# Attention and a routed expert layer on one Trainium2 core: list weights behind first products, three routing buffers, four small gate products, and a new order

## The chip, the cores and the metric

The kernel runs on one core of one Trainium2 chip. The metric is the device time of one execution in microseconds (us). The engines are TensorE (PE), VectorE (DVE), ScalarE (ACT), GpSimd (POOL) and SyncE (SP), which issues DMA transfers; each runs its own list of instructions in a fixed order and waits for others by semaphores.

## The reference, cut to what matters

```
a = softmax(phi, over the sequence)                 # 8 batches, 8 heads, 576 tokens, 32 memory slots
k_m, v_m = a^T k, a^T v
x = softmax(q k_m^T / 8) v_m                        # x: 4608 tokens x 512
noisy = x Wg + log1p(exp(x Wn)) * noise             # 8 experts
top2 and softmax of their two values
for each expert e, each of its tokens t:
    out[t] += weight[t, e] * relu(x[t] W1[e]) W2[e]   # W1 512 x 1024, W2 1024 x 512
```

## The kernel before, in words

The 64 batch-heads are 16 units of one batch and four heads (`unit`, `a_load` to `a_v`): load phi, k and v, form exp, k_m and v_m, and scores of q. Batches go in four pairs P0 to P3 of 1152 tokens, nine tiles of 128 rows and five groups n each (`JS`, `group`). A group is put through transposes (`c_sc`), softmax (`c_soft1`, `c_soft2`; L396 is the last multiply, by 1/sum), transposes (`c_tr`) and the products with v (`c_av`), which leave a tile of x in `xr`; ACT copies it from PSUM (L419) and SP writes it to a DRAM buffer `xs` (L423). The same product brings the gate logits as 16 more columns: `a_g` has multiplied each unit's v by the gate's weights (L318), masked the result to the diagonal blocks of the four heads (L320) and summed it over the heads (L322).

When a pair is complete, `gate` (P3 in two parts, five tiles and four) finds each token's two experts on DVE (to `gmb`, L474), counts places in the experts' lists by products on PE (L480 to L485), turns these into `gidx` (L502), has POOL number the tokens (iota, L495) and DVE the weights in `gent`, and scatters one list entry a token and choice to the DRAM list `lst`: 72 scatters on POOL (L514), 18 a pair, the last pair 10 and 8. A list read (L593, on SP) waits for the scatters of the pairs that it needs.

Experts then run over their lists: POOL gathers 128 rows of x (`gtile`, L640), ACT and DVE split them into two f16 halves (`ghalf`, L651 and L654, a ring of two buffers), SP transposes them by DMA (L655). `mm1` makes the first products (L678, PSUM ring `mp` of three), ACT the relu `r` (L684), DVE the halves hh and hl (L685, L686). `mm2` makes the second products (L705, L715), ACT scales them by the list weights `wlu` to `y` (L709), and POOL adds them to `out` (L728), which SP has zeroed in 38 writes (L150). Weights are loaded (L544), measured (`wam`, L555), scaled (`wsc`) and split into halves wh and wl (L569, L570).

Expert 0 has groups g0, g1 (two tiles each, which need only P0 and P1), g2 (two tiles, needs P2) and (0,3) (four tiles, the last of 64 entries, needs all lists). They run while attention still does; experts 1 to 7 follow in groups of 4, 4 and 2 tiles. `wt` makes `wlu`: L617 for whole tiles, L621 for the 64 entries.

The order of work before (0,3) comes from a list of tasks sorted by times that the table `PRI` gives; a scheduler places instructions of each engine by these. `BUF` holds ring sizes, and numbers that tie an instruction behind a named product (`after`). Behind it the program's own order of calls counts. What stands first on an engine runs first; nothing passes a waiting instruction on its engine.

## Time and profile before

| | |
|---|---|
| median of 3 runs | 1042.14 us (1041.88 to 1044.54) |
| profiled execution, its own time | 1048.34 us |
| its span | 1046.5 us |
| mean granted clock of TensorE, share of full speed | 0.958 |
| busy in the span: PE, DVE, ACT, POOL | 92%, 51%, 35%, 29% |
| chain that ended last, by engine | PE 56%, DMA 8%, issue 6%, DVE 6%, POOL 2% |

The span runs from the first to the last instruction that the profile shows; the execution's own time is 1.8 us longer. A row of a timeline gives the start and the length of an instruction (or of several alike), and in brackets how long its engine stood idle before and what ended that. A window's row gives each engine's busy time in a stretch. Idle time of an engine matters only if the chain passes through it.

### The profile page before, as it was taken

Reading aid. Unit: us, or ns where it says so; the run is one execution under the profiler, and the core shown is the slowest. Engines: PE = TensorE matmul, PEld = TensorE weight load, DVE = VectorE, ACT = ScalarE, POOL = GpSimd, SP = SyncE. Lnnn points to the kernel's source line nnn. Section 1 sums busy time; section 2 is a strip of 40 time slices with the busy share of each in tenths; the row PEclk is TensorE's granted clock in tenths of the full one; section 3 lists DMA queues with packets and bytes.
Section 4 is the critical chain, followed back from the end, with each engine's and each line's share of the span. In section 5 each row is a group of like instructions: output and inputs, shape, how many; then the busy total and the mean of one; then the engine's idle time right before and its main releaser. Section 6 shows DMA issues by size and latency. Waiting matters only on the chain.

```text
span 1046.5 us, 15053 instructions
## 1 busy us (share of the span) xinstructions
PE 962.7 (92%) x5632; PEld 500.4 (48%) x5632; DVE 535.2 (51%) x1395; ACT 370.5 (35%) x760; POOL 298.4 (29%) x262
## 2 busy tenths in 40 slices
PE   4898975895799998999999999999999999999995
PEld 3555643563344445444644464445444544454452
DVE  2578888535476254984272349544523682232211
ACT  3466655313242232532242244324222542221211
POOL 1000633776246304222323132223132213211121
PEclk9699977798899999999999999999999999999998
DMA  9999999555988439756546257845453626430221
GB/s 291 331 327 327 267 330 302 113 118 84 238 148 196 95 37 176 204 129 100 107 131 110 42 91 206 170 88 82 131 101 78 124 57 110 66 51 11 31 32 25
DMA packets 143642, 147.93 MB, mean 141 GB/s; under 512 B 92944, under 2 KB 102224, under 8 KB 143568
## 3 DMA queue, kind: packets, MB, share of 16 engines
q1 hardware_dynamic: 124112, 107.02, 39.9%
q0 software_dynamic: 19456, 39.93, 22.0%
q8 instruction: 45, 0.74, 0.3%
q14 instruction: 29, 0.24, 0.1%
HBM read 86.77 MB, written 40.22 MB: 121 GB/s over the span
## 4 chain that ended last, share of the span: by engine, by line
PE 56%; DMA 8%; issue 6%; DVE 6%; POOL 2%; ACT 1%; SPq 0%; POOLq 0%; ACTq 0%; DVEq 0%
PE mp L678 27%; PE ps L705 27%; DMA xt<-ghalf 3%; DVE wl L570 2%; DMA lst<-gent,gidx 2%; DVE wam L555 2%; PE ps L715 2%; DMA stg<-in_w 2%; DMA out<-y,lt 1%; POOL out L728 1%; POOL lst L514 1%; DVE ghalf L654 1%; DVE hl L686 0%; ACT ghalf L651 0%; DVE hh L685 0%
## 5 line engine op out<-in xcount | busy, mean ns | idle before, releaser
L678 PE MATMUL mp<-xt,wh 128*128 128x512 f16 (+2 forms) x1408 | 280.2, 336 | 11.3 <-issue 6.6
L678 PEld LDWEIGHTS <-wh 128*128 128x128 f16 x1600 | 152.5, 99 | 143.6 <-issue 26.6
L728 POOL DMA_INDIRECT out<-y,lt x80 | 128.7, 1609 | 259.8 <-ACT y L709 231.9
L705 PE MATMUL ps<-wh,hl 128*128 128x512 f16 x528 | 200.0, 379 | 1.6 <-DVE hl L686 1.6
L705 PE MATMUL ps<-wl,hh 128*128 128x512 f16 x528 | 199.8, 379 | 0.0
L685 DVE CAST hh<-r 128x512 f16<-128x512 f32 (+3 forms) x200 | 72.1, 364 | 248.8 <-ACT r L684 247.7
L705 PE MATMUL ps<-wh,hh 128*128 128x512 f16 x528 | 195.5, 379 | 1.3 <-DVE hh L685 1.3
L640 POOL DMA_INDIRECT gtile<-xs,lt x80 | 91.0, 1138 | 332.5 <-DVE ghalf L654 292.0
L684 ACT ACTIVATE r<-mp 128x512 f32<-128x512 f32 (+3 forms) x200 | 97.0, 492 | 246.9 <-PE mp L678 175.4
L705 PEld LDWEIGHTS <-hh 128*128 128x128 f16 x1152 | 112.3, 98 | 135.1 <-DVE hh L685 4.6
L678 PE MATMUL mp<-xt,wl 128*128 128x512 f16 (+2 forms) x704 | 151.4, 337 | 0.0
L654 DVE TENSOR_TENSOR ghalf<-gtile,ghalf 128x512 f16<-128x512 f32 x80 | 55.1, 691 | 126.1 <-ACT ghalf L651 125.9
L686 DVE TENSOR_TENSOR hl<-r,hh 128x512 f16<-128x512 f32 (+3 forms) x200 | 111.3, 562 | 4.6
L651 ACT ACTIVATE ghalf<-gtile 128x512 f16<-128x512 f32 x80 | 50.0, 628 | 170.7 <-DMA xt<-ghalf 155.6
L514 POOL DMA_INDIRECT lst<-gent,gidx x72 | 73.0, 1014 | 129.3 <-DVE pe L385 102.8
L678 PEld LDWEIGHTS <-wl 128*128 128x128 f16 x800 | 76.9, 99 | 58.6 <-issue 1.3
L705 PEld LDWEIGHTS <-hl 128*128 128x128 f16 x576 | 56.3, 98 | 74.7 <-issue 5.7
L555 DVE TENSOR_REDUCE wam<-stg 128x1 f32<-128x512 f32 x128 | 81.1, 678 | 20.4 <-DMA stg<-in_w 20.2
L709 ACT ACTIVATE y<-ps,wlu 128x512 f32<-128x512 f32 x66 | 44.7, 681 | 125.0 <-PE ps L705 92.0
L570 DVE SCALAR_TENSOR_TENSOR wl<-stg,wsc,wh 128x512 f16<-128x512 f32 x112 | 76.4, 743 | 1.9 <-ACT wh L569 1.7
L569 ACT ACTIVATE wh<-stg,wsc 128x512 f16<-128x512 f32 x112 | 70.1, 708 | 14.2 <-DVE wsc L336 13.8
L417 PE MATMUL xp<-vb,at 128*128 128x272 f32 (+1 forms) x160 | 50.6, 477 | 14.7 <-ACT xr L419 14.0
(160 smaller groups left out, 723.2 us busy)
## 6 DMA issues: line engine op xcount, KB each, us to landing
stg<-in_w SPq DMA_DIRECT2D x64, 512.0 KB
kvs<-in_kv SPq DMA_DIRECT2D x16, 1024.0 KB
out<-zt SPq DMA_DIRECT2D x38, 256.0 KB
qs<-in_q_t SPq DMA_DIRECT2D x16, 576.0 KB
xs<-xr SPq DMA_DIRECT2D x36, 256.0 KB
phs<-in_phi_t SPq DMA_DIRECT2D x16, 288.0 KB
kvs<-in_kv SPq DMA_DIRECT2D x16, 128.0 KB
gtile<-xs,lt POOLq DMA_INDIRECT x80
```

Of the source, the lines that this page charges most:

```text
L514: sc = G.indirect_dma_start(out=lst[:, :], out_offset=bass.IndirectOffsetOnAxis(ap=idx[:, j, k:k + 1], axis=0), in_=ent[:, j, k, :], in_of ...
L555: d = V.tensor_reduce(am[:, c:c + 1], ss[c], axis=AX.X, op=OP.max, apply_absolute_value=True)
L569: A.activation(wh[:, cs], ss[c], AF.Identity, scale=sc)
L570: V.scalar_tensor_tensor(wl[:, cs], ss[c], sc, wh[:, cs], op0=OP.mult, op1=OP.subtract)
L640: G.indirect_dma_start(out=gts[i][:n], out_offset=None, in_=xs[0:seen, :], in_offset=bass.IndirectOffsetOnAxis(ap=LT[e][:n, t, 0:1].bitcas ...
L654: V.tensor_tensor(gh[:n, 1], gts[i][:n], gh[:n, 0], OP.subtract)
L678: d = mark["mm1", g if e == 0 else None] = T.matmul(ps[:, :n], ww[:, c * FF + f * 128:c * FF + (f + 1) * 128], xt[:, xo + c, :n], start=(k ...
L684: A.activation(r[:, :n], ps[:, :n], AF.Relu, scale=HC)
L685: V.tensor_copy(hh[:, f, :n], r[:, :n])
L686: V.tensor_tensor(hl[:, f, :n], r[:, :n], hh[:, f, :n], OP.subtract)
L705: T.matmul(ps, hs[:, i * 128:(i + 1) * 128], ws, start=(k == 0), stop=(k == 8 * m - 1))
L728: d = G.indirect_dma_start(out=out[:, :], out_offset=bass.IndirectOffsetOnAxis(ap=LT[e][:n, t, 0:1].bitcast(I32), axis=0), in_=y[:n], in_o ...
```

## The change

The table `PRI` and some numbers of `BUF` are set anew, and the ring of gathered tiles has four buffers, not three. `a_g` makes four products of 32 rows by 16 columns, one for each head, side by side in one PSUM tile, and ACT copies the result; DVE's mask and sum go. The last multiply of the softmax is on GpSimd for the first five groups (`GL` and `GV` are zero, so their branches change nothing). `gidx` and `gent` have three buffers, not one. `early_wt`'s tie behind the first product of its group now holds for all tiles of expert 0, and the list weights of (0,3) are made behind that group's first products, not before its gathers. Line numbers of the changed kernel are 2 to 7 higher.

```diff
-PRI = dict(D=5.51308, p=-3.88947, kv=-1.28633, q=-2.43825, exp=-1.09034, tr1=-2.82213, tr5=-2.85978, kvm=0.71326,
...
+PRI = dict(D=5.82512, p=-2.56477, kv=-1.63998, q=-2.4532, exp=-1.09005, tr1=-2.82213, tr5=-2.85978, kvm=0.91616,
...
-           ws=1, m0=16, m1=18, m2=19, r0=6, r1=6, zr=5)
+           ws=1, m0=15, m1=18, m2=19, r0=14, r1=3, zr=6)
-GT = 3
+GT = 4
+GN, GL, GV = 5, 0, 0
@@ a_g
-        T.matmul(p4[:, 0, 0:64], VT[u], wg_sb[:, g, :], start=True, stop=True)
-        gt = sm.tile([128, 4, 16], F32, name="gt")
-        V.tensor_tensor(gt, p4[:, 0, 0:64].rearrange("p (h c) -> p h c", h=4), vmask[:, :, 0:16], OP.mult)
         vb = wk.tile([128, 272], F32, name="vb", bufs=8)
-        V.tensor_reduce(vb[:, 256:], gt.rearrange("p h c -> p c h"), axis=AX.X, op=OP.add)
+        for h in range(4):
+            T.matmul(p4[h * 32:(h + 1) * 32, 0, 0:16], VT[u][:, h * 32:(h + 1) * 32],
+                     wg_sb[:, g, h * 16:(h + 1) * 16], start=True, stop=True)
+        A.activation(vb[:, 256:], p4[:, 0, 0:16], AF.Copy)
@@ c_soft2
-        V.tensor_tensor(pe[:, 0:k], pe[:, 0:k], ss[:, 0:k, None].to_broadcast([128, k, M]), OP.mult)
+        (G if n < GN else V).tensor_tensor(pe[:, 0:k], pe[:, 0:k], ss[:, 0:k, None].to_broadcast([128, k, M]), OP.mult)
@@ gate
-        idx = gs.tile([128, NJ, 2], I32, name="gidx")
-        ent = gs.tile([128, NJ, 2, 2], F32, name="gent")
+        idx = gs.tile([128, NJ, 2], I32, name="gidx", bufs=3)
+        ent = gs.tile([128, NJ, 2, 2], F32, name="gent", bufs=3)
@@ wt
-        if e == 0 and t1 <= 6:
+        if e == 0:
             after(d, "mm1", t0 // 2)
@@ the main sequence
     lists(0, 6, NTL + 1)
-    wt(0, 6, NTL + 1)
...
         for f in range(8):
             mm1(e, g, f)
             step_side(2)
+        if (e, g) == (0, 3):
+            wt(0, 6, NTL + 1)
```

**POOL, from ahead of P2's scatters to P3's last.** Before:

```order
L495 IOTA gent 128x18
L640 DMA gtile<-xs,lt 128x512 x3
L514 DMA lst<-gent,gidx 37888x2 x13
L640 DMA gtile<-xs,lt 128x512
L514 DMA lst<-gent,gidx 37888x2 x5
L495 IOTA gent 128x10
L514 DMA lst<-gent,gidx 37888x2 x10
L728 DMA out<-y,lt 4864x512
L640 DMA gtile<-xs,lt 128x512 x2
L728 DMA out<-y,lt 4864x512
L495 IOTA gent 128x8
L514 DMA lst<-gent,gidx 37888x2 x8
```

After the change (L520 is the scatter, L646 the gather, L734 the add to `out`):

```order
L501 IOTA gent 128x8
L646 DMA gtile<-xs,lt 128x512 x4
L520 DMA lst<-gent,gidx 37888x2 x28
L646 DMA gtile<-xs,lt 128x512 x2
L734 DMA out<-y,lt 4864x512 x2
L520 DMA lst<-gent,gidx 37888x2 x8
L646 DMA gtile<-xs,lt 128x512 x3
```

P2's 18 scatters and the first 10 of P3 stand in one run behind four gathers; the gather in P2's scatters and the iotas between them are gone from there.

**SP, around the first list reads** (L150 zero writes, L423 and L429 x tiles, L593 and L599 list reads). Before:

```order
L150 DMA out<-zt 128x512 x5
L423 DMA xs<-xr 256x1x256 x2
L150 DMA out<-zt 128x512
L423 DMA xs<-xr 256x1x256
L150 DMA out<-zt 128x512 x2
L593 DMA lt<-lst 128x2x2 x2
L423 DMA xs<-xr 256x1x256 x2
L655 DMA_TRANSPOSE stg<-ghalf 128x8x128 x2
```

After the change:

```order
L152 DMA out<-zt 128x512
L429 DMA xs<-xr 256x1x256
L152 DMA out<-zt 128x512
L599 DMA lt<-lst 128x2x2 x2
L152 DMA out<-zt 128x512 x4
L429 DMA xs<-xr 256x1x256
L152 DMA out<-zt 128x512 x2
L429 DMA xs<-xr 256x1x256 x4
L661 DMA_TRANSPOSE stg<-ghalf 128x8x128 x2
```

The list reads stand ahead of the last six zero writes and of four x tiles that they stood behind.

**ACT and DVE, in g1 and g2.** ACT before, from g1's r's to the first r's of g2 with the first two halves of (0,3) (L684 and L690 are r, L651 and L657 halves, L709 and L715 y, L569 wh):

```order
L684 ACTIVATE r<-mp 128x256 x7
L651 ACTIVATE ghalf<-gtile 128x512
L684 ACTIVATE r<-mp 128x256
L651 ACTIVATE ghalf<-gtile 128x512
L709 ACTIVATE y<-mp,wlu 128x512 x2
L569 ACTIVATE wh_3813<-stg,wsc 128x512 x3
L684 ACTIVATE r<-mp 128x256
L569 ACTIVATE wh_3813<-stg,wsc 128x512 x5
L651 ACTIVATE ghalf<-gtile 128x512
L684 ACTIVATE r<-mp 128x256
L651 ACTIVATE ghalf<-gtile 128x512
L684 ACTIVATE r<-mp 128x256 x4
```

ACT after the change, from g2's first half on:

```order
L657 ACTIVATE ghalf<-gtile 128x512
L690 ACTIVATE r<-mp 128x256
L657 ACTIVATE ghalf<-gtile 128x512
L690 ACTIVATE r<-mp 128x256 x3
L575 ACTIVATE wh_3829<-stg,wsc 128x512 x8
L690 ACTIVATE r<-mp 128x256 x3
L657 ACTIVATE ghalf<-gtile 128x512 x2
L715 ACTIVATE y<-mp,wlu 128x512 x2
L690 ACTIVATE r<-mp 128x256
L657 ACTIVATE ghalf<-gtile 128x512
L690 ACTIVATE r<-mp 128x256
L657 ACTIVATE ghalf<-gtile 64x512
```

g2's two halves follow r 9 and r 10, and the halves of (0,3) stand ahead of g1's y's and among the first r's of g2. DVE after the change, at the end of g1's halves (L627 are the list weights of the 64 entries, L660 the halves of gathered tiles, L691 and L692 hh and hl):

```order
L691 CAST hh<-r 128x256 x2
L692 TENSOR_TENSOR hl<-r,hh 128x256 x2
L691 CAST hh<-r 128x256
L627 TENSOR_SCALAR wlu<-lt,wu 64x1
L692 TENSOR_TENSOR hl<-r,hh 128x256
L660 TENSOR_TENSOR ghalf<-gtile,ghalf 128x512 x2
L691 CAST hh<-r 128x256
L692 TENSOR_TENSOR hl<-r,hh 128x256
L660 TENSOR_TENSOR ghalf<-gtile,ghalf 128x512
```

The 64 entries' weights, which stood behind DVE's scale chain, now stand ahead of g1's last hl.

## Rows read from the trace of the kernel before

**Rows 1.** The page, part 1: engine, busy us, share, instructions.

```profile
PE 962.7 (92%) x5632; PEld 500.4 (48%) x5632; DVE 535.2 (51%) x1395; ACT 370.5 (35%) x760; POOL 298.4 (29%) x262
```

**Rows 2.** Table of windows: length, busy us of each engine (instructions), PEclk, DMA share, GB/s.

```profile
150.00:175.00 25.00, 18.19 (x85) 10.66 (x82) 22.93 (x78) 17.31 (x41) 14.90 (x15) 0.88 1.07 299
196.05:208.60 12.55, 12.55 (x106) 10.58 (x107) 8.33 (x46) 3.05 (x10) 9.51 (x10) 0.85 0.52 69
208.60:219.40 10.80, 10.80 (x60) 5.11 (x59) 4.45 (x26) 1.91 (x5) 6.51 (x8) 1.00 0.27 32
325.00:1046.00 721.00, 704.25 (x3728) 343.79 (x3726) 327.58 (x675) 225.37 (x397) 177.54 (x132) 1.00 0.50 97
```

**Rows 3.** Timeline of PE: start, us, line, operation, [idle before <-releaser].

```profile
24.61 1.43 PE L275 MATMUL tr<-kvs,es 128*32 128x128 f32 x40 [0.76 <-DMA kvs<-in_kv]
...
255.65 1.01 PE L678 MATMUL mp<-stg,wh 128*128 128x256 f16 x4 [5.61 <-ACT r L684]
...
285.60 1.65 PE L678 MATMUL mp<-xt,wh 128*128 128x448 f16 x4 [6.65 <-issue]
```

**Rows 4.** Timeline of POOL, 168 to 254 us.

```profile
168.01 0.97 POOL L514 DMA_INDIRECT lst<-gent,gidx  x1 [0.30 <-issue]
...
184.83 1.00 POOL L640 DMA_INDIRECT gtile<-xs,lt  x1 [9.79 <-DMA lt<-lst]
...
188.66 1.00 POOL L514 DMA_INDIRECT lst<-gent,gidx  x1 [0.30 <-issue]
...
214.73 0.14 POOL L495 IOTA gent<- 128x10 int32 x1 [1.79 <-DMA lst<-gent,gidx]
...
228.46 1.62 POOL L728 DMA_INDIRECT out<-y,lt  x1 [0.30 <-DMA lst<-gent,gidx]
...
246.14 1.62 POOL L728 DMA_INDIRECT out<-y,lt  x1 [0.30 <-issue]
253.28 1.01 POOL L640 DMA_INDIRECT gtile<-xs,lt  x1 [5.51 <-DMA lt<-lst]
```

**Rows 5.** Timeline of SP (its DMA queue), 179 to 268 us.

```profile
179.30 1.09 SPq L593 DMA_DIRECT2D lt<-lst  x2
...
189.71 3.26 SPq L655 DMA_TRANSPOSE stg<-ghalf  x2
...
247.81 10.50 SPq L593 DMA_DIRECT2D lt<-lst  x16
...
261.07 6.45 SPq L655 DMA_TRANSPOSE xt<-ghalf  x2
```

**Rows 6.** Timeline of ACT, the halves of gathered tiles.

```profile
194.79 0.63 ACT L651 ACTIVATE ghalf<-gtile 128x512 f16<-128x512 f32 x1 [1.42 <-DMA stg<-ghalf]
...
258.56 0.61 ACT L651 ACTIVATE ghalf<-gtile 128x512 f16<-128x512 f32 x1
...
271.03 0.63 ACT L651 ACTIVATE ghalf<-gtile 128x512 f16<-128x512 f32 x1 [5.79 <-DMA xt<-ghalf]
...
275.80 0.63 ACT L651 ACTIVATE ghalf<-gtile 64x512 f16<-64x512 f32 x1 [3.59 <-DMA xt<-ghalf]
```

**Rows 7.** Timeline of DVE, the waits around routing and list weights.

```profile
182.46 0.18 DVE L502 CAST gidx<-gai 128x18 int32<-128x18 f32 x1
...
232.68 0.17 DVE L502 CAST gidx<-gai 128x8 int32<-128x8 f32 x1 [6.83 <-DMA lst<-gent,gidx]
...
252.36 0.23 DVE L617 TENSOR_SCALAR wlu<-lt,wu 128x3 f32<-128x3 f32 x1 [9.85 <-DMA lt<-lst]
```

**Rows 8.** Groups of instructions: xcount, busy us, mean ns of one, idle before, releasers.

```profile
L514 POOL DMA_INDIRECT lst<-gent,gidx x72 | 73.0, 1014 | 129.3 <-DVE pe L385 102.8 <-issue 20.1 <-DVE vb L322 4.7
...
L396 DVE TENSOR_TENSOR pe<-pe,ss 128x512 f32<-128x512 f32 (+1 forms) x20 | 12.6, 632 | 0.1
...
L322 DVE TENSOR_REDUCE vb<-gt 128x16 f32<-128x64 f32 x16 | 4.0, 252 | 0.0
...
L320 DVE TENSOR_TENSOR gt<-tr,vmask 128x64 f32<-128x64 f32 x16 | 3.5, 221 | 4.1 <-PE tr L318 4.0
```

More of the change, by code (lines that the diff above doesn't have):

```diff
@@ L30 @@
 ZERO_AT = 20
-PRI = dict(D=5.51308, p=-3.88947, kv=-1.28633, q=-2.43825, exp=-1.09034, tr1=-2.82213, tr5=-2.85978, kvm=0.71326,
-           kt=0.96429, s=2.13563, g=1.7535, v=4.20111, v1=2.31831, sc=-2.03055, s1=-0.23727, s2=0.32735, tr=-0.49952,
-           av=1.31436, avb=1.42743, gate=0.6, g2=1.60082, gs=0.99413, x0=0.3, md=0.403, md1=0.00959, fill=5.02228,
-           prep=2.87573, prd=0.4427, wl=1.48361, wl3=3.40386, pr1=2.97844, z=4.13465, zd=0.20212, d0=-0.08768,
-           d1=-0.27982, d2=0.09897, d3=-0.24281, sc0=-0.181, sc1=0.0, sc2=0.47741, sc3=0.10255, f0=1.2075, f1=0.2,
-           g0=0.94365, g1=0.42741, prep0=4.0, prd0=0.43318)
+PRI = dict(D=5.82512, p=-2.56477, kv=-1.63998, q=-2.4532, exp=-1.09005, tr1=-2.82213, tr5=-2.85978, kvm=0.91616,
+           kt=0.96429, s=2.13563, g=2.0709, v=4.2088, v1=2.62186, sc=-2.24007, s1=-0.02984, s2=0.281, tr=-0.49952,
+           av=1.31436, avb=1.42743, gate=0.6, g2=0.5622, gs=0.99413, x0=0.22977, md=0.48714, md1=0.34264,
+           fill=5.44306, prep=2.87573, prd=0.4427, wl=1.24791, wl3=3.40386, pr1=5.96246, z=4.13465, zd=0.20212,
+           d0=-1.41967, d1=-0.24329, d2=0.08664, d3=-0.00869, sc0=0.16753, sc1=0.0, sc2=-0.03774, sc3=0.12087,
+           f0=-0.09359, f1=0.2, g0=1.24719, g1=0.39992, prep0=3.62472, prd0=0.55109)
 BUF = dict(kvs=3, phs=3, qs=2, et=2, es=3, pe=4, at=3, xr=4, st0=1, st1=1, ptr=3, px=2, mps=3, xa=3, w1=8, w2=8, zg=9,
-           ws=1, m0=16, m1=18, m2=19, r0=6, r1=6, zr=5)
+           ws=1, m0=15, m1=18, m2=19, r0=14, r1=3, zr=6)
 NEED = (1, 1, 2)
-GT = 3
+GT = 4
 HC = 2.0 ** -14
 WEXP = 2.0 ** 9
+GN, GL, GV = 5, 0, 0
 SBITS = float((2 * 127 + 9) << 23)
@@ L357, in a_v @@
             vm = VM[2 * b + g]
-            V.scalar_tensor_tensor(vb, vm[:, None, :].to_broadcast([128, 4, D]), s, vmask, op0=OP.mult, op1=OP.mult)
+            if b < GV:
+                G.tensor_scalar(vm, vm, s, None, op0=OP.mult)
+                G.tensor_tensor(vb, vm[:, None, :].to_broadcast([128, 4, D]), vmask, OP.mult)
+            else:
+                V.scalar_tensor_tensor(vb, vm[:, None, :].to_broadcast([128, 4, D]), s, vmask, op0=OP.mult, op1=OP.mult)
     JS = ((0, 1), (2, 3), (4,), (5, 6), (7, 8))
@@ L423, in c_av @@
         nc.sync.dma_start(xs[r0:r0 + 128, :].rearrange("p (g d) -> p g d", g=2), xr[:, :, 0:256])
-        V.tensor_tensor(LG[P][:, j], xr[:, 0, 256:], xr[:, 1, 256:], OP.add)
+        (G if n < GL else V).tensor_tensor(LG[P][:, j], xr[:, 0, 256:], xr[:, 1, 256:], OP.add)
     scatters, reads, gated = [], [], set()
```

## The prediction

> **What bounds the kernel now.** I read the page's first part, then the table of windows, then the timelines of PE, POOL, SP, DVE and ACT where PE stands idle. TensorE is busy for 962.7 us of 1046.5 [rows 1]: what spares another engine matters only if it shortens one of PE's pauses or brings PE's steady part forward. The windows tell where these are [rows 2]. In 150 to 175 us the DMA share is 1.07 at 299 GB/s and DVE is busy for 22.93 of 25 us, PE for 18.19. After 325 us PE is busy for 704.25 of 721 us with DMA at 0.50: that stretch is PE's own, and its order hardly changes. So a gain must be a shift of the moment at which expert 0's last group, (0,3), starts. Before it PE waits 6.65 us and starts at 285.60 [rows 3]; the row says "issue", but the tiles it multiplies come through a chain that the other timelines show.
>
> That chain runs through GpSimd [rows 4]. P1's scatters end at 168.01 + 0.97; the gathers of the first group wait 9.79 us for a list read and run from 184.83; P2's scatters start behind them at 188.66; P3's second part ends at 246.14, where the next row starts; the gathers of (0,3) start at 253.28. The list read that held the first gathers was issued by SyncE at 179.30, the last ones from 247.81 [rows 5]. From there on gathered tiles go through ACT, DVE and transposes. The buffer of halves has two places, so a third half waits until a transpose has read the first: the transpose issued at 261.07 [rows 5] lets ACT go on at 271.03 [rows 6], 10.0 us later; the one issued at 189.71 lets it go on at 194.79, 5.1 us later. The fourth half follows 4.8 us behind the third (275.80).
>
> **The change, part by part.**
>
> *List weights.* The weights of (0,3)'s list entries stood in front of DVE's scale chain and now stand behind (0,3)'s first products. That wait was 9.85 us [rows 7]; behind it stood the new weights' halves, ACT's r, and PE, which lost 5.61 us [rows 3]. Worth alone: nothing, since PE then waits 6.65 us for (0,3) in any case. It counts only if (0,3)'s data come sooner too. And one row escapes: the weights of the last tile's 64 entries carry no such gate, and DVE's new order has them **ahead of g1's last hl**. They need the same list read, so DVE now stops there, earlier than it did; that hl waits behind it, and for the hl PE's second products of g1 (third step).
>
> *Three routing buffers.* The gidx of P3's second part waited 6.83 us for scatters [rows 7], and the iota at 214.73 waited 1.79 us for P2's landing [rows 4]. With three buffers both waits go. On PE the first is again covered by the 6.65 us; on POOL the 1.79 us go from the chain.
>
> *Four small products for one, and an ACT copy.* DVE loses 16 x (0.22 + 0.25) = 7.5 us [rows 8]. ACT gains 16 copies, each between nothing and the 0.63 us of a 128x512 one [rows 6]; I take 0.3, nearer the bottom as they have 16 columns, 5 us in all, in a front where ACT is busy 17.31 of 25 us [rows 2]: zero, and 5 us if ACT had no room. PE issues eight instructions for two. Forty small products take 1.43 us, 36 ns each [rows 3], so eight take 0.3 us: zero.
>
> *Five multiplies on GpSimd.* DVE loses 5 x 0.63 = 3.2 us [rows 8]. No row shows this operation on GpSimd. Its price lies between DVE's 0.63 us and, as an outer bound, the 1.62 us of POOL's longest row here [rows 4]; I take 1.3, nearer the top as no row shows GpSimd as fast as DVE. POOL idles 102.8 us ahead of the first scatters [rows 8], so 5 x 1.3 = 6.5 us hide there; without that cover they cost up to 8 us. [...]
>
> *The order.* This carries the forecast. First step: the first list reads stand on SP behind 32 zero writes and P2's last x tile; before, they stood behind all 38 and four x tiles more. Ten transfers of 256 KB, 2.6 MB at 299 GB/s [rows 2], are 8.8 us, so they issue at about 171 instead of 179.30: −8. They also need P1's scatters, which ended at 169 and whose gate now stands a tile earlier. The gathers follow 5.5 us later (179.30 to 184.83), at 176.5, four instead of three, 5.1 us long. P2's scatters need their gidx as well, at 182.46 before [rows 7]; its gate stands a tile earlier, but its last x tile, counted in bytes along SP's order, comes 1.3 MB (4 us) later: 182 to 184. So P2 starts at about 183.5, −5.
>
> Second step: P2 and the first part of P3 are now 28 scatters in one run. A step is 1.28 us (184.83 to 188.66 is three, 188.66 to 214.73 less 1.79 is nineteen), so they end at 219.5; before they ended at 228.46, being cut by a gather and the iota. That is −9. Two gathers, two outs and eight scatters follow as before, 17.7 us (228.46 to 246.14): P3 ends at 237, the last list reads go at 239, the gathers of (0,3) at 244.3, all −9. P3's first gidx must be there by 206.5; its gate now stands behind 54 of g0's first products. 96 of these move as many columns as the 48 second products of a group, which take 10.80 us [rows 2], so it comes 6 us after g0's start near 192, and 4 us of DVE later, at 202, in time.
>
> Third step, the price: ACT's order has the halves of later groups **ahead** of r's and y's. g2's first half stands right behind r 9, so the r's of g1 wait for a gather that lands near 223; PE, with three buffers, stops 3 to 4 us and ends g1's first products at 192 + 12.55 + 10.80 + 10.8 + 3.5 = 229.5 [rows 2]. After 22 of g1's second products (5 us, 234.5) it lacks the last hl, behind DVE's new wait, which ends when the lists land, 5 us after 239: PE stops until 244.5, 10 us, and the other 26 products (5.9 us) end at 250.4. The first two halves of (0,3) come 5.3 us after the gather (253.28 to 258.56), at 249.6, ahead of g1's two y's, so r 17 follows at 252 and no buffer is short. Then come the third half, r 18, the fourth, and the rest. With 5.1 us for a transpose the third half comes at 255.5 and holds nobody: g2's first products end at 250.4 + 10.8, its second ones (10.80 us) at 272. With 10.0 us and 4.8 us the third half comes at 260.5, r 19 at 266, three more first products of 1.35 us and the second ones end at 281. (0,3)'s own transposes land at 263.5 or 276, earlier. So (0,3) starts at 272 to 281 instead of 285.60: −13.6 to −4.6. I take −9, the middle: the weight loads that shared the time with these transposes now stand behind the first two, but the reads of all lists lie right ahead. Expert 1's second weights are made later, behind r's of (0,3); they cost nothing while PE has eight first products of (1,0) to do before it wants them.
>
> **Sum.** The profiled execution's own time is 1048.34 us, 6.2 above the median of 1042.14. Less 9 it is 1039.3; the median becomes 1033. A difference of 0.3%, 3.1 us, is about what a measurement of this kernel can tell from no change.
>
> **Rivals.**
> *B, more.* DVE loses 10.7 us in the front, and in 150 to 175 us it is busy 92%. If DVE rather than DMA holds the front, most of that comes on top: −9 − 9 = −18, 1024. For it: PE has room there (18.19 of 25) and DVE has not. Against: DMA at 1.07 in the same window.
>
> *C, nothing.* The lists come 5 us earlier, not 9 (gidx of P2 late, as its gate sits in the dense stretch of DVE), and transposes take 10 us: 290 − 5 = 285 against 285.6, 1041.5. Or the change does not do what it says: the wait for the list weights is back as the 64 entries' wait, and the one for scatters was covered by the 6.65 us: 1042.
>
> *D, slower: ACT held.* One mechanism, the halves that stand ahead of y's and r's on ACT. From (0,3)'s first half on, the steps above take 22.4 us with quick transposes and 31.4 with slow ones. If that half comes at 258.56 as before, they end at 281 or 290. So with slow transposes it is slower from a lead of the lists under 4.5 us on, at most by 4.5 us, 1046.5; with transposes of 13 us from a lead of 9 already. For it: ACT already idles for transposes (5.79 and 3.59 us [rows 6]). [...]
>
> **How the numbers follow.** Forecast 0.45, B 0.20, C 0.16, D 0.19. Forecast and B are faster, C is same: faster 0.65, same 0.16, slower 0.19. The forecast's own range is 1028.5 to 1037.5. The whole range takes in B with all of DVE's relief and some of PE's pauses (−25, 1017) and D to 1047.
>
> **What would show it.** Right: first list reads near 171, 28 scatters without a gap ending near 219, (0,3)'s gathers near 244, a DVE wait for the list in front of the 64 entries' weights, ending near 244, with a PE pause beside it, (0,3)'s first product between 272 and 281, the stretch after it as long as before. Wrong: list reads at 179 or later; P2's scatters waiting for gidx; g2's end after 285; or a longer stretch after (0,3)'s start, which would say that expert 1's weights or tiles come late.

## The result and the profile after

The changed kernel takes 1029.47 us (median of 4 runs, 1027.66 to 1036.48) beside 1042.46 us for the kernel before in the same runs (median of 4, 1041.88 to 1044.54): a ratio of 0.988, 95% interval 0.985 to 0.991, or 13.0 us less. The forecast was 1033 us, 9 less. Here and below, medians leave out two single executions in a slower state of the chip (the kernel before at 1119.80 us beside the first group of runs, `e8_no_relief` at 1304.83 us).

The profiled execution took 1027.66 us (span 1025.9). It lies 1.8 us below its median, and that of the kernel before lay 5.9 above its own, so the two profiled executions differ by 20.7 us, of which the medians bear out 13.0; the other 7.7 are the spread of single executions. The rows below tell where the time moved, the medians how much.

Page, part 1, after (answers to [rows 1]: PE's busy time fell by 17.6 us, DVE's by 6.4):

```profile
PE 945.1 (92%) x5728; PEld 490.7 (48%) x5728; DVE 528.8 (52%) x1358; ACT 372.4 (36%) x776; POOL 289.9 (28%) x267
```

Table of windows, after: one for [rows 2], then the span cut at the moments that the prediction speaks of, which are the start of g0's first product (188.67), of (0,3)'s (267.92) and of its last second product (310.78). Columns: length, then busy us of PE, PEld, DVE, ACT, POOL with counts, PEclk, DMA share, GB/s.

```profile
150.00:175.00 25.00, 15.90 (x57) 8.90 (x55) 22.25 (x80) 14.19 (x32) 4.99 (x7) 0.77 1.06 327
0.00:120.00 120.00, 89.45 (x1010) 56.45 (x1010) 73.87 (x263) 69.57 (x203) 28.18 (x52) 0.96 0.98 316
120.00:188.67 68.67, 47.91 (x363) 28.95 (x363) 56.17 (x212) 38.76 (x97) 29.60 (x30) 0.83 0.99 307
188.67:267.92 79.25, 68.19 (x456) 44.55 (x456) 45.07 (x154) 23.57 (x53) 48.84 (x47) 0.96 0.70 162
267.92:310.78 42.86, 37.04 (x191) 17.36 (x191) 20.02 (x39) 12.27 (x22) 14.80 (x14) 1.00 0.87 147
310.78:1025.90 715.12, 702.48 (x3713) 343.42 (x3709) 333.66 (x693) 228.20 (x401) 168.45 (x126) 0.99 0.48 98
```

The same cuts in the kernel before (g0 at 196.05, (0,3) at 285.60, its last second product at 327.72):

```profile
0.00:120.00 120.00, 96.71 (x921) 61.13 (x922) 75.44 (x281) 65.95 (x183) 13.93 (x35) 0.89 0.98 314
120.00:196.05 76.05, 54.32 (x361) 33.21 (x360) 61.52 (x241) 41.46 (x106) 37.13 (x39) 0.78 1.00 280
196.05:285.60 89.55, 70.54 (x451) 45.00 (x452) 42.30 (x144) 22.08 (x49) 51.46 (x48) 0.90 0.68 129
285.60:327.72 42.12, 39.56 (x197) 18.52 (x199) 30.49 (x63) 15.74 (x28) 20.78 (x11) 0.96 0.93 195
327.72:1046.50 718.78, 701.53 (x3706) 342.52 (x3702) 325.43 (x670) 225.32 (x396) 175.12 (x131) 1.00 0.50 96
```

At 120 us both kernels have moved about as much (316 and 314 GB/s). Then the stretch to g0's first product is 7.4 us shorter, with the same bytes moved at its end (120 x 316 + 68.67 x 307 is 59.0 MB, 120 x 314 + 76.05 x 280 also 59.0 MB). Cut once more, at the first list reads, it shows where these bytes went (two rows after the change, then two before):

```profile
120.00:168.05 48.05, 35.08 (x302) 20.85 (x302) 39.53 (x150) 26.39 (x68) 17.95 (x19) 0.88 1.02 318
168.05:188.67 20.62, 12.82 (x61) 8.11 (x61) 16.64 (x63) 12.37 (x30) 11.65 (x11) 0.70 0.91 280
120.00:179.30 59.30, 44.05 (x319) 26.78 (x318) 53.00 (x195) 35.25 (x89) 28.36 (x30) 0.83 1.08 306
179.30:196.05 16.75, 10.27 (x42) 6.43 (x42) 8.52 (x46) 6.22 (x17) 8.78 (x9) 0.60 0.73 184
```

Up to the list reads DMA is full in both, at 318 and 306 GB/s. By then 53.2 MB have moved after the change and 55.8 before, so the list reads passed 2.6 MB, as forecast. Behind them DMA is busier than it was (0.91 against 0.73): the passed transfers are moved there. From g0 to (0,3) another 10.3 us go, 8.0 of them PE's idle time (19.0 to 11.1) and 2.4 busy time at a higher granted clock (0.96 against 0.90). (0,3) itself is 0.7 us longer, the rest of the program 3.7 shorter. So the gain is there before (0,3) starts, as forecast.

The chain, engine by engine. POOL, after (answers to [rows 4]):

```profile
172.91 1.45 POOL L646 DMA_INDIRECT gtile<-xs,lt  x1 [11.24 <-DMA out<-zt]
...
179.48 1.00 POOL L520 DMA_INDIRECT lst<-gent,gidx  x1 [1.37 <-DVE gidx L508]
...
214.62 0.96 POOL L520 DMA_INDIRECT lst<-gent,gidx  x1 [0.30 <-DMA lst<-gent,gidx]
...
231.77 1.26 POOL L520 DMA_INDIRECT lst<-gent,gidx  x1 [0.30 <-issue]
237.76 0.97 POOL L646 DMA_INDIRECT gtile<-xs,lt  x1 [4.73 <-DMA lt<-lst]
```

The 28 scatters from 179.48 to 214.62 have only 0.30 us between them. The row of 172.91 names a zero write as what ended the wait; in the program a gather needs its list and tiles of x, not a zero write, and the list reads were issued just ahead of that write, so I read the wait as the list's. SP (answers to [rows 5]) and DVE (answers to [rows 7]):

```profile
168.05 1.07 SPq L599 DMA_DIRECT2D lt<-lst  x2
...
234.88 9.02 SPq L599 DMA_DIRECT2D lt<-lst  x16
244.00 2.64 SPq L661 DMA_TRANSPOSE xt<-ghalf  x2
```

```profile
179.03 0.17 DVE L508 CAST gidx<-gai 128x18 int32<-128x18 f32 x1
...
217.99 0.16 DVE L508 CAST gidx<-gai 128x8 int32<-128x8 f32 x1
...
237.27 0.20 DVE L627 TENSOR_SCALAR wlu<-lt,wu 64x1 f32<-64x1 f32 x1 [2.79 <-DMA lt<-lst]
```

The gidx of P3's second part no longer waits (6.83 us before). The list's wait on DVE stands in front of the 64 entries' weights, as forecast, but is 2.79 us long and ends at 237. ACT (answers to [rows 6]) and PE (answers to [rows 3]):

```profile
221.36 0.63 ACT L657 ACTIVATE ghalf<-gtile 128x512 f16<-128x512 f32 x1 [8.52 <-DMA gtile<-xs,lt]
...
241.29 0.63 ACT L657 ACTIVATE ghalf<-gtile 128x512 f16<-128x512 f32 x1 [7.14 <-DMA gtile<-xs,lt]
...
247.85 0.63 ACT L657 ACTIVATE ghalf<-gtile 128x512 f16<-128x512 f32 x1 [2.88 <-DMA xt<-ghalf]
...
251.37 0.63 ACT L657 ACTIVATE ghalf<-gtile 64x512 f16<-64x512 f32 x1 [2.62 <-DMA xt<-ghalf]
```

```profile
218.60 0.32 PE L331 MATMUL pb<-identf,wam 128*128 128x128 f32 x1 [2.31 <-DVE wam L567]
222.31 1.01 PE L684 MATMUL mp<-stg,wh 128*128 128x256 f16 x4 [3.39 <-ACT r L690]
...
244.17 0.60 PE L684 MATMUL mp<-stg,wh 128*128 128x256 f16 x4 [1.20 <-ACT y L715]
...
252.32 0.60 PE L684 MATMUL mp<-stg,wh 128*128 128x256 f16 x4 [2.04 <-ACT r L690]
...
267.92 0.92 PE L684 MATMUL mp<-xt,wh 128*128 128x448 f16 x4
```

ACT waits 8.52 us for the gather of g2's first half, and g1's r's stand behind it, the first at 221.90. So PE has no first product to run from 216.29 to 222.31, 6.0 us: 2.31 and 3.39 us idle around one small product (`pb`), which waits for DVE's wam. Behind this stop PE's granted clock is half for 5.9 us:

```profile
222.31:228.24 5.93, 5.93 (x29) 4.07 (x28) 5.66 (x17) 3.94 (x8) 4.71 (x5) 0.50 1.11 143
```

ACT's wait for the gathers of (0,3), 7.14 us, costs PE 1.20 for a y. The third half comes 3.85 us after the transposes were issued at 244.00, and PE loses 2.04 us beside the fourth.

(0,3)'s first product has no wait in front of it: PE comes straight from g2. Its data were there earlier. The ring of halves has two places, so the second half of (1,0) can only be made when the transpose of (0,3)'s fourth tile has read its place. That half ran at 285.62 before the change, the moment at which PE started (285.60), and at 262.04 after it, 5.9 us ahead of PE:

```profile
285.62 0.63 ACT L651 ACTIVATE ghalf<-gtile 128x512 f16<-128x512 f32 x1 [3.31 <-DMA xt<-ghalf]
...
262.04 0.62 ACT L657 ACTIVATE ghalf<-gtile 128x512 f16<-128x512 f32 x1
```

Before, (0,3) waited for its data; after the change it waits for PE to be done with g0 to g2. Groups of the new operations, shapes apart (count | busy us, mean ns | idle before):

```profile
L402 DVE TENSOR_TENSOR pe<-pe,ss 128x512 f32<-128x512 f32 x12 | 8.2, 684 | 0.1
...
L322 PE MATMUL tr<-wg_sb,vt 64*32 64x16 f32 x128 | 4.6, 196 | 1.7 <-ACT vt L296 1.7
...
L402 POOL TENSOR_TENSOR pe<-pe,ss 128x512 f32<-128x512 f32 x4 | 4.2, 1048 | 38.6 <-ACT vb L324 28.4 <-ACT es L288 4.4 <-DVE ss L401 3.3
...
L324 ACT ACTIVATE vb<-tr 128x16 f32<-128x16 f32 x16 | 2.9, 179 | 1.2 <-PE tr L322 1.2
```

### The profile page after: what moved, and what is told of

The parts are those of the page before. It is cut to its first block, busy times and chain, and to the rows that moved or that the text cites. A ratio compares the mean times of both kernels' runs of the same rounds, so it can differ in the third digit from the quotient of the medians.

```text
span 1025.9 us, 15234 instructions
## 1 busy us (share of the span) xinstructions
PE 945.1 (92%) x5728; PEld 490.7 (48%) x5728; DVE 528.8 (52%) x1358; ACT 372.4 (36%) x776; POOL 289.9 (28%) x267
## 4 chain that ended last, share of the span: by engine, by line
PE 69%; DMA 13%; DVE 5%; issue 5%; ACT 3%; POOL 2%; SPq 1%; POOLq 0%; ACTq 0%
PE mp L684 30%; PE ps L711 29%; DMA xt<-ghalf 4%; DMA stg<-in_w 3%; PE ps L721 2%; PE xp L312 2%; PE xp L423 2%; DMA phs<-in_phi_t 2%; DVE wl L576 1%; PE tr L277 1%; POOL out L734 1%; DMA out<-y,lt 1%; POOL lst L520 1%; DMA kvs<-in_kv 1%; DVE wam L561 1%
## 5 line engine op out<-in xcount | busy, mean ns | idle before, releaser
L684 PE MATMUL mp<-xt,wh 128*128 128x512 f16 (+2 forms) x1408 | 279.9, 336 | 3.0 <-ACT r L690 1.7
L684 PEld LDWEIGHTS <-wh 128*128 128x128 f16 x1600 | 151.6, 98 | 132.1 <-issue 14.4
L734 POOL DMA_INDIRECT out<-y,lt x80 | 127.4, 1593 | 283.8 <-ACT y L715 251.9
L691 DVE CAST hh<-r 128x512 f16<-128x512 f32 (+3 forms) x200 | 71.7, 362 | 241.3 <-ACT r L690 240.1
L690 ACT ACTIVATE r<-mp 128x512 f32<-128x512 f32 (+3 forms) x200 | 96.7, 491 | 232.4 <-PE mp L684 156.2
L646 POOL DMA_INDIRECT gtile<-xs,lt x80 | 79.8, 998 | 315.0 <-DVE ghalf L660 272.2
L684 PE MATMUL mp<-xt,wl 128*128 128x512 f16 (+2 forms) x704 | 150.4, 336 | 0.0
L660 DVE TENSOR_TENSOR ghalf<-gtile,ghalf 128x512 f16<-128x512 f32 x80 | 55.0, 689 | 124.4 <-ACT ghalf L657 124.3
L692 DVE TENSOR_TENSOR hl<-r,hh 128x512 f16<-128x512 f32 (+3 forms) x200 | 111.4, 562 | 4.8
L657 ACT ACTIVATE ghalf<-gtile 128x512 f16<-128x512 f32 x80 | 50.1, 628 | 173.7 <-DMA xt<-ghalf 154.4
L684 PEld LDWEIGHTS <-wl 128*128 128x128 f16 x800 | 76.1, 98 | 57.4
L715 ACT ACTIVATE y<-ps,wlu 128x512 f32<-128x512 f32 x66 | 44.8, 681 | 130.5 <-PE ps L711 87.3
L520 POOL DMA_INDIRECT lst<-gent,gidx x72 | 72.2, 1002 | 66.1 <-DVE gidx L508 32.0
L423 PE MATMUL xp<-vb,at 128*128 128x272 f32 (+1 forms) x160 | 46.6, 441 | 13.3 <-ACT xr L425 10.8
## 6 DMA issues: line engine op xcount, KB each, us to landing
kvs<-in_kv SPq DMA_DIRECT2D x16, 128.0 KB, 11.3
```

Of the source, the lines that this page charges most:

```text
L423: mark["av", n] = T.matmul(xp[lo:hi, 0:272], at[:, 2 * i + g, lo:hi], VB[2 * b + g], start=True, stop=True)
L520: sc = G.indirect_dma_start(out=lst[:, :], out_offset=bass.IndirectOffsetOnAxis(ap=idx[:, j, k:k + 1], axis=0), in_=ent[:, j, k, :], in_of ...
L646: G.indirect_dma_start(out=gts[i][:n], out_offset=None, in_=xs[0:seen, :], in_offset=bass.IndirectOffsetOnAxis(ap=LT[e][:n, t, 0:1].bitcas ...
L684: d = mark["mm1", g if e == 0 else None] = T.matmul(ps[:, :n], ww[:, c * FF + f * 128:c * FF + (f + 1) * 128], xt[:, xo + c, :n], start=(k ...
L690: A.activation(r[:, :n], ps[:, :n], AF.Relu, scale=HC)
L691: V.tensor_copy(hh[:, f, :n], r[:, :n])
```

## The experiments

The runs stand in three groups; those of a group share a chip and the runs of the kernel before. That kernel took 1091.85 us beside the first group, 1043.29 beside the second (as in the result), 1092.65 beside the third. Only runs of one group are compared. Ratios are to the kernel before; moments in us are from each profile:

```
group                      median  ratio [95%]            lists1  g0     lists2  gather (0,3)   end    span
before (result)            1042.46 1                      179.30  196.05 247.81  253.28 285.60  327.72 1046.5
after (result)             1029.47 0.988 [0.985, 0.991]   168.05  188.67 234.88  237.76 267.92  310.78 1025.9
1      b0_before           1094.98 one run                208.44  226.24 292.43  296.81 328.80  371.48 1093.2
       a0_after            1065.59 0.977 [0.973, 0.980]   188.83  212.15 270.10  273.08 305.26  347.68 1066.1
       e1_order_only       1083.19 0.993 [0.990, 0.996]   193.44  216.79 282.88  285.88 314.49  363.46 1080.8
       e2_parts_old_order  1080.64 0.991 [0.988, 0.994]   206.57  222.40 292.84  299.32 323.07  363.99 1079.8
2      a1_after            1032.98 0.991 [0.988, 0.993]   168.81  189.60 236.54  239.82 271.45  312.87 1028.4
       e3_list_reads_late  1048.16 1.005 [1.002, 1.008]   180.74  199.65 248.17  251.70 283.65  328.53 1043.7
       e4_no_act_hold      1035.05 0.992 [0.989, 0.995]   171.70  192.85 239.53  242.99 272.51  319.95 1035.9
       e5_one_routing_b.   1044.11 1.000 [0.998, 1.003]   169.42  192.97 240.73  244.03 273.36  332.36 1045.7
3      a2_after            1066.33 0.977 [0.974, 0.980]   190.32  213.99 273.00  276.36 307.10  349.15 1065.2
       e6_weights_behind_t 1073.79 0.982 [0.978, 0.986]   188.68  212.96 268.52  271.43 310.79  356.61 1074.8
       e7_list_weights_e.  1065.79 0.976 [0.973, 0.980]   189.47  212.64 272.85  275.86 307.07  349.04 1063.4
       e8_no_relief        1074.53 0.984 [0.980, 0.987]   195.97  219.38 280.42  283.58 310.94  359.36 1074.9
```

"lists1" is the issue of the first list reads, "g0" that group's first product, "lists2" the issue of the last list reads, "gather" the first gather of (0,3), "(0,3)" its first product, "end" its last second product. From "end" to the span's end it is 713 to 722 us in all fourteen, whatever the edit: nothing that was tried works behind (0,3).

**The kernels unchanged**, `b0_before`, `a0_after` and `a2_after`, and `a1_after` in the second group.

> The kernel before, unchanged, for a second profile of it. Both theories: a time near 1042 us. The first profile was an execution of 1048.3 us, 6 above the median. If the slow transposes (10 us for the first one of group (0,3)) and the start of (0,3) at 285.6 us belong to the kernel, they are here again; if they were that execution's own, this profile has (0,3) start some 4 to 6 us earlier.

> The changed kernel, unchanged, as the reference for the runs beside it: 0.988 of before, 1029 to 1030 us, first list reads near 168 us, gathers of (0,3) near 238, its first product near 268.

> The changed kernel again, as the reference for the three beside it, since the run of before and after depends on the chip that a group of runs gets: 0.976 to 0.990 of before. The three beside it are read against this one.

> The changed kernel again, as the reference for the three beside it on their chip: 0.976 to 0.991 of before.

The gain is there on every chip: 10.3 us (0.9%) in the second group, 26.3 us (2.3%) in the first and third. The last section returns to the difference. What `b0_before` was to settle, whether the slow transposes and the start of (0,3) at 285.60 belong to the kernel, it can't: the kernel before is 50 us slower on its chip. For the same reason `a0_after` missed its expected 1029 us.

**The order alone, and the parts alone.** `e1_order_only` is the kernel before with the new `PRI` and `BUF`; `e2_parts_old_order` is the changed kernel with the old ones.

```diff
@@ e1, against before
-           ws=1, m0=16, m1=18, m2=19, r0=6, r1=6, zr=5)
+           ws=1, m0=15, m1=18, m2=19, r0=14, r1=3, zr=6)
@@ e2, against after
-           ws=1, m0=15, m1=18, m2=19, r0=14, r1=3, zr=6)
+           ws=1, m0=16, m1=18, m2=19, r0=6, r1=6, zr=5)
...
```

(`PRI` goes with it in both.)

> The kernel before with the new table of times and tie numbers alone: one routing buffer, the old gate product, DVE's multiply, list weights ahead of the gathers, three gather buffers. First list reads stand 3.7 MB earlier on SP than before, but GpSimd's run is still cut by iotas and a gather. Theory L (the end follows the list chain: list reads, scatters, gathers of (0,3), transposes): the reads come at about 167 us, the gathers of (0,3) about 7 to 9 us earlier than before, time 0.992 to 0.995, more than half of the gain. Theory F (the gain comes from DVE and ACT being relieved in the front by the code parts): no gain, 0.998 to 1.002.

> All code parts of the change (four small products, GpSimd multiplies, three routing buffers, four gather buffers, list weights behind first products) with the old table of times and tie numbers. First list reads stand on SP behind all 38 zero writes as before, but the 28 scatters are one run. Theory L: list reads near 177 to 179 us, P2's scatters 2 to 4 us earlier than before, the gathers of (0,3) 4 to 6 us earlier, time 0.994 to 0.998. Theory F: nearly the whole gain, 0.988 to 0.991, with the first product of g0 near 189 us.

The order alone gave 8.7 us (1083.19 against 1091.85), the parts alone 11.2, both together 26.3. With the order alone the first list reads come 15.0 us earlier than before (193.44 against 208.44), with the parts alone 1.9. But the order alone loses 6 us of its 14 inside (0,3), which takes 49.0 us (314.49 to 363.46) against 42 in the kernels before and after.

The parts alone do not gain through the list chain. Their last list reads come 0.4 us later than in `b0_before` and the gathers 2.5 later, and still (0,3) starts 5.7 us earlier, 23.8 us behind the gathers instead of 32.0. Between the gathers and (0,3) PE waits 1.59 and 0.60 us there, and 2.73, 2.38, 0.28, 4.02 and 2.91 us in `b0_before`. No run tells which part does this; the list weights, made behind (0,3)'s first products, and the fourth gather buffer both bear on that stretch.

The two gains add up to 19.9 of 26.3 us, so some of the gain needs both. The forecast, which gave the parts 1.79 us, had them wrong on this chip.

**The list reads put back.** In the changed kernel the first list reads are tied behind the last zero write, and the first group is placed later.

```diff
+            mark["z", c // ZC] = d
...
+            if e == 0 and t0 < 4:
+                after(d, "z", 37)
...
-                gate_at[-1], busy = early(0, g, gate_at[-1] + PRI["x0"], max(w_at, zeroed, busy), PRI["md"])
+                gate_at[-1], busy = early(0, g, gate_at[-1] + PRI["x0"] + (6.0 if g == 0 else 0.0), max(w_at, zeroed, busy), PRI["md"])
```

> The changed kernel with the first list reads put back where they stood before on SP, behind all 38 zero writes and four more x tiles (2.6 MB later), all else of the change kept. Theory L (the end follows the list chain): the first gathers come 6 to 10 us later, P2's scatters, the last list reads and the start of (0,3) by as much less the 1 to 2 us that GpSimd had to spare ahead of P2's scatters; time 5 to 9 us above the changed kernel. Theory F (the relief of DVE and ACT in the front makes the gain): less than 3 us.

SP in `e3_list_reads_late`:

```profile
180.74 1.89 SPq L600 DMA_DIRECT2D lt<-lst  x2
...
248.17 9.38 SPq L600 DMA_DIRECT2D lt<-lst  x16
257.66 17.25 SPq L664 DMA_TRANSPOSE xt<-ghalf  x6
```

The reads go at 180.74, 11.9 us later than in `a1_after`; the last list reads come 11.6 later, the gathers 11.9, (0,3) 12.2, and the time is 15.2 us longer (1048.16 against 1032.98): the whole gain, and 5 us more, where 5 to 9 us were expected. A delay here is passed on nearly one to one to (0,3). The edit also gives g0 a later place, but that is not what delays it: its first product, 10.1 us later than in `a1_after`, waits for its own transposes.

```profile
199.65 1.01 PE L687 MATMUL mp<-stg,wh 128*128 128x256 f16 x4 [8.08 <-DMA stg<-ghalf]
```

So the first step of the forecast is shown: the first list reads set the start of (0,3). Two ways lead there from these reads, through the last lists and gathers (11.9 us later) and through g0's products on PE (10.1 later), and this run moves both.

**Two holds taken away, one on ACT and one on DVE.** The first half of (0,3) is tied behind g2's first r, so that g1's y's and that r stand ahead of it; the 64 entries' weights stand behind (0,3)'s first products. The hold by g2's first half stays (ACT waits 8.46 us there).

```diff
-            V.tensor_scalar(wu[0:TAIL, NTL:], LT[e][0:TAIL, NTL:, 1], W[k, 2][0:TAIL], None, op0=OP.mult)
+            d = V.tensor_scalar(wu[0:TAIL, NTL:], LT[e][0:TAIL, NTL:, 1], W[k, 2][0:TAIL], None, op0=OP.mult)
+            if e == 0:
+                after(d, "mm1", t0 // 2)
...
+            elif (e, g) == (0, 3) and i == 0:
+                after(d, "g2f0")
...
+        if (e, g, f) == (0, 2, 0):
+            mark["g2f0",] = d
```

> The changed kernel with its two new holds taken away: the first halves of (0,3) stand on ACT behind g1's two y's and the first r of g2 instead of ahead of them, and the weights of the 64 entries stand behind (0,3)'s first products. The forecast's third step (these holds stop PE by about 19 us, of which the lateness of (0,3)'s data hides a part): g2 ends earlier and (0,3) starts when its transposes land, 3 to 8 us before the changed kernel's start; time 3 to 8 us below it. Rival: the holds stop PE only while the lists are late and the lists are now early, so PE has 1 to 3 us to gain at most and the transposes come that much later: within 3 us of the changed kernel.

Nothing was gained, as the rival had it: 1035.05 against 1032.98, with intervals that overlap. The front of `e4_no_act_hold` is also some 3 us later from the list reads on, so the stretch that lost its holds, from "lists2" to (0,3), is read by its length: 33.0 us against 34.9 in `a1_after`. About 2 us lay there, and (0,3) itself then took 47.4 us, not 41.4: what was gained ahead of it was given back inside. The third step's price of 10 us was not being paid.

**One routing buffer.** `gidx` and `gent` without `bufs=3`.

```diff
-        idx = gs.tile([128, NJ, 2], I32, name="gidx", bufs=3)
-        ent = gs.tile([128, NJ, 2, 2], F32, name="gent", bufs=3)
+        idx = gs.tile([128, NJ, 2], I32, name="gidx")
+        ent = gs.tile([128, NJ, 2, 2], F32, name="gent")
```

> The changed kernel with one buffer for gidx and gent, as before: the run of 28 scatters is cut again by an iota, which waits for P2's entries to land, and P3's second part by another. Theory L: 2 to 4 us later lists, time 2 to 4 us above the changed kernel; P3's second gidx waits again, up to 7 us on DVE, hidden behind the wait for the lists. Theory F: the same as the changed kernel, within 1 us.

The time is 11.1 us longer than `a1_after`, all of the gain, where 2 to 4 us were expected. The wait that the buffers remove costs what the chain says: gathers 4.2 us later, (0,3) 1.9 later. The rest is inside (0,3), 59.0 us long against 41.4. ACT and PE there:

```profile
272.79 1.19 ACT L657 ACTIVATE ghalf<-gtile 128x512 f16<-128x512 f32 x2 [9.43 <-DMA xt<-ghalf]
...
286.54 0.63 ACT L657 ACTIVATE ghalf<-gtile 128x512 f16<-128x512 f32 x1 [10.12 <-DMA xt<-ghalf]
```

```profile
293.08 1.65 PE L684 MATMUL mp<-xt,wh 128*128 128x448 f16 x4 [10.48 <-ACT r L690]
...
327.86 0.64 PE L721 MATMUL ps<-wh,hh 128*64 128x512 f16 x2 [5.29 <-ACT y L715]
```

ACT waits 9.43 and 10.12 us for transposes, and PE 10.48 us for the r's behind them and later 5.29 us for a y. The first are D's mechanism, ACT held by halves, at a place that D did not name. Which of the buffers' effects lets it in, the later lists or the weight loads that then stand otherwise between the transposes, this run does not separate.

**Weight loads put behind the transposes.** One theory for such waits is that weight loads between the transposes slow them. The first weights of expert 2 were tied behind (0,3)'s first products.

```diff
+            elif (e, i) == (2, 0):
+                after(d, "mm1", 3)
```

> The changed kernel with expert 2's first weights tied behind (0,3)'s first products, so that on SP all four transposes of (0,3) and two of expert 1's stand ahead of any weight load; before that, four loads of 512 KB stood between the second and the third. Theory T (a transpose that is issued behind weight loads lands late, 8 to 14 us instead of 4, and the ring of two halves then holds ACT and PE; that is where the run with one routing buffer lost its time): ACT's waits for transposes in (0,3) and g2 fall under 4 us each, (0,3) starts 2 to 4 us earlier and its first products have no pause over 3 us; time 3 to 7 us below the changed kernel. Rival (transposes take what they take, or expert 2's weights then come late): within 3 us of the changed kernel, or above it.

It was 7.5 us slower than `a2_after` (1073.79 against 1066.33), where the theory wanted 3 to 7 us less. The gathers came 4.9 us earlier, but (0,3) 3.7 later: the third half's successors still waited, with the weight loads away. SP and ACT:

```profile
277.65 22.29 SPq L663 DMA_TRANSPOSE xt<-ghalf  x6
300.02 2.47 SPq L550 DMA_DIRECT2D stg<-in_w  x4
```

```profile
295.94 0.63 ACT L659 ACTIVATE ghalf<-gtile 128x512 f16<-128x512 f32 x1 [6.39 <-DMA xt<-ghalf]
...
317.09 0.63 ACT L659 ACTIVATE ghalf<-gtile 128x512 f16<-128x512 f32 x1 [9.72 <-DMA xt<-ghalf]
```

With six transposes in one run and no load between them, ACT still waits 6.39 us, and 9.72 for a later one (6.85 and 8.14 in `a2_after`). As posed the theory falls. The test is not clean, since the scheduler also put halves of (1,0) ahead of g2's last r's, and PE waits 4.78 us for an r there.

**The list weights put back early.** `wt` as it was, all else new.

```diff
-        if e == 0:
+        if e == 0 and t1 <= 6:
...
+    wt(0, 6, NTL + 1)
...
-        if (e, g) == (0, 3):
-            wt(0, 6, NTL + 1)
```

> The changed kernel with the list weights of (0,3) made ahead of its gathers again, without the tie, as before. In the order they then stand on DVE beside the 64 entries' weights, at the end of g1's halves. The forecast (the tied row only moved a wait, since the 64 entries' row waits for the same list read at the same place): within 2 us of the changed kernel. Rival (this part is what the change is named for and carries it): 4 us or more above the changed kernel.

1065.79 against 1066.33: no difference. In this order those weights stand on DVE beside the 64 entries' row (275.53 and 276.02), and on this chip neither waits for the list; in the result that row waited 2.79 us. So the part that names the change first is worth nothing here. With the old order it was not tested apart.

**DVE's relief taken back.** The old `a_g`, and `GN` 0.

```diff
-GN, GL, GV = 5, 0, 0
+GN, GL, GV = 0, 0, 0
...
+        T.matmul(p4[:, 0, 0:64], VT[u], wg_sb[:, g, :], start=True, stop=True)
...
-        for h in range(4):
...
-        A.activation(vb[:, 256:], p4[:, 0, 0:16], AF.Copy)
+        V.tensor_reduce(vb[:, 256:], gt.rearrange("p h c -> p c h"), axis=AX.X, op=OP.add)
```

> The changed kernel with the old gate product (DVE masks and sums) and the softmax's last multiply on DVE throughout, order table, routing buffers, gather buffers and list weights as changed. Theory F (relief of DVE in the front, 10.7 us of busy time, makes a good part of the gain): the front and the first product of g0 come 4 to 8 us later, time 5 to 10 us above the changed kernel. Theory L (DMA holds the front, the list chain the rest): the first list reads come within 3 us of the changed kernel's and the time stays within 3 us.

8.2 us slower than `a2_after` (1074.53 against 1066.33), in the 5 to 10 us of theory F: the list reads come 5.7 us later, g0 5.4, the gathers 7.2, (0,3) 3.8, and (0,3) takes 6.4 us more. That is rival B's mechanism, a front that follows DVE, seen on this chip. But the scheduler moves other instructions too when these parts go, and the run was not made on a chip like the result's, so 8.2 us is neither the relief's price alone nor B's price there.

No version beat the changed kernel: `e7_list_weights_early` and `e4_no_act_hold` cannot be told from it.

## Why the prediction was right, and where its steps were off

**The mechanism.** Right in its main line: the gain is an earlier start of (0,3), and it hangs on the first list reads (`e3_list_reads_late`). The way from there is the forecast's only in part. The last lists and gathers come earlier, and that frees (0,3) from its wait for data; how early it starts is then set by g0's start and PE's stops. And (0,3)'s own length, which the forecast took as unchanged, grows by 6 to 18 us in `e1_order_only`, `e4_no_act_hold` and `e5_one_routing_buffer` (47 to 59 us against 41 to 43): an early start is not enough.

1029.47 lies in the forecast's own range, 3.5 us below its middle. In part that is luck. On PE's way to (0,3) g0 began 3.3 us ahead of the forecast, what followed up to g1's second products took 5.0 us more, these took 10.5 less, and g2 4.8 more: errors of both signs that leave 4.1 us against the forecast's early end (272). In the order of the prediction's steps:

*First step.* List reads at 168.05, forecast 171: −11.3, not −8. The term counted the bytes rightly (2.6 MB, 8.6 us at 306 GB/s). That 0.24 MB more would be moved by 120 us (0.8 us), and that DMA would run at 318 instead of 306 GB/s from there to the list reads (1.9 us), stood in no term. First gathers 172.91 (176.5), P2's scatters 179.48 (183.5): −9.2, not −5. Its gidx came at 179.03, where counting bytes had put it at 182 to 184, and POOL waited 1.37 us for it.

*Second step.* 28 scatters in 36.1 us (179.48 to 215.58), forecast 36; P3's end at 233.0, four us ahead of the forecast, all of it inherited from the first step. From there to the last list reads 1.9 us (2 forecast). The read-to-gather gap was mis-sized: 2.88 us, forecast 5.3. It is 2.9 to 3.5 us in all eleven profiles with the new order, and 5.5, 4.4 and 6.5 us in the three with the old one, where an add to `out` stands on POOL right ahead of these gathers. So the gathers moved by −15.5, not −9.

*Third step, the price.* This is the step that failed. The stop at g1 took 6.0 us, forecast 3 to 4, and the half clock behind it (5.9 us long, so an estimated 3.0 us lost) stood in no term. The 10 us for the 64 entries' wait did not come: DVE's wait was 2.79 us and ended at 237.27, not 244.5, while PE ran g1's second products from 231.14 to 241.50 without a pause. The lists were read 4 us earlier than forecast and landed 2.4 us after the first read's issue, not 5; PE's second products began 1.6 us later; what was left PE's other products covered. So g1's second products ended at 241.50, not 250.4. Part of this was given back in g2, whose products took 26.4 us, not 21.6, with waits of 1.20, 0.54, 2.04 and 1.05 us on PE. The third half came at 247.85, not 255.5 to 260.5: it came 3.85 us after the transposes' issue, below both bounds (5.1 and 10.0). In `a1_after` that took 7.6 us and PE lost 4.08 for an r, and even so (0,3) started without a wait. `e4_no_act_hold`, without the 64 entries' hold, gained nothing. So (0,3) starts at 267.92 (271.45 in `a1_after`), ahead of the forecast's 272 to 281: −17.7 by these two profiles, of which their spread is a part; by medians the whole gain is 13.0.

**The parts.** *List weights*: worth nothing with the new order, as forecast (`e7_list_weights_early`). *The fourth gather buffer* had no term, and no run takes it back alone. *Three routing buffers*: the term was 1.79 us, and taking them back costs 11.1. The term had the wait on POOL right in kind and missed that the order built on three buffers holds ACT inside (0,3) without them. *Small products and copies*: eight products of a unit are busy for 4.6 / 16 = 0.29 us (0.3 forecast), a copy for 0.179 us (0.3 estimated). *GpSimd's multiplies*: 1.048 us for 128x512, forecast 1.3, and DVE's own 0.684, so 1.53 times; 0.617 against 0.415 for 128x256. The five took 4.8 us, not 6.5. POOL idles 38.6 us ahead of these four 128x512 ones, so the cover that the forecast named is there. *DVE's relief* was put at zero in the forecast and at −9 in B. `e8_no_relief` puts it at 8.2 us on a chip where DMA is not full ahead of g0 (share 0.85 to 120 us and 0.83 from there in `a2_after`, against 0.98 and 0.99). On the result's chip it was not measured; DVE is still busy for 22.25 of 25 us from 150 to 175 us there (22.93 before).

**The rivals.** C fell with the list reads at 168.05 and the gathers 15.5 us earlier. D fell here: the lists' lead is 13 us and the transposes were quick. On ACT r's did wait behind a half before the change: the two of 271.57 ran straight behind the half of 271.03, though PE's last product for them had ended at 267.42. D's waits are real in `e5_one_routing_buffer` too (9.43 and 10.12 us), but (0,3) is as long after the change as before (42.9 and 42.1 us). B is not decided: more was gained than the forecast's 9, but a front that DVE holds is seen only in `e8_no_relief`, and on the result's chip DMA was full up to the list reads (1.02) as it was before (1.08). The stretch after (0,3) is as long as before, 715.1 against 718.8 us, as the prediction's last sign wanted.

**Still open.** Why DMA moved 318 instead of 306 GB/s from 120 us to the list reads; how the parts alone bring (0,3) nearer to its gathers; why one routing buffer makes (0,3) 59 us long; and B's price on the result's chip.

## What to carry to other kernels

When PE is 92% busy, find the one start that the steady part hangs on and follow its chain through all queues: here a list read, 28 scatters and a gather on engines that the busy shares call idle, where a delay of 11.9 us came back almost whole. Then ask again what holds that start: here it was data before the change and PE's own earlier products after it. A wait worked out as the difference of two forecast moments carries the errors of both: 244.5 less 234.5 made a stop of 10 us, and each end was off by enough to leave none. A buffer or a helper that looks worth its own wait alone can be what an order set for it rests on: undo it with the order in place before calling it small.
